# A gated mix of a recurrent memory layer and full attention: its list scheduler rewritten, leftover rows in partition halves, one read for four segments

## The chip, the core and the metric

The kernel runs on one core of a Trainium2 chip. The core has a matrix engine (TensorE; PE for its matmuls and PEld for its weight loads), VectorE (DVE), ScalarE (ACT), GpSimd (POOL), and SyncE (SP), which issues transfers. Engines run their own instruction lists in order and wait for each other through semaphores. PE reads SBUF and writes PSUM, which has eight banks; 16 DMA engines move data between the memory of the chip and SBUF. The metric is the device time of one execution in microseconds (us).

## The reference

Two layers read the same 2048 x 576 input and are mixed row by row with a gate g.

```python
g = sigmoid((x * gate_w).sum(-1, keepdims=True))
# A: 64 segments of 32 rows, each with 8 memory rows in front (h has 40 rows)
for s in range(n_seg):
    h = concatenate([mem, x[:, 32 * s:32 * s + 32]], axis=1)
    q, k, v = h @ Wq, h @ Wk, h @ Wv                  # 32 heads of 128
    scores = where(mask, q @ k.T * scale, -1e9)       # memory rows see all, the rest is causal
    o = (softmax(scores) @ v) @ Wo                    # summed over heads
    mem = o[:, :8]                                    # the next segment's memory
    outs.append(o[:, 8:])
# B: full attention, 32 heads of 18, over all 2048 rows
b = softmax(q @ k.T * scale) @ v @ wo
return g * a + (1 - g) * b
```

Layer A is a recurrence: a segment's first 8 output rows go into the next segment's projections. Layer B has no order among its parts. Operands are bfloat16.

## The kernel before, in words

**Two kinds of work on one set of engines.** The recurrence of A has a long chain of small steps per segment. B consists of 512 *visits*: each takes 128 keys, 512 queries and four heads. In a visit PE multiplies keys and queries in four row tiles of 32 (`sb`, L935; three results in one three-bank tile `sb`, the fourth in a bank `sp`), ScalarE takes the exponentials (`ex`, `ey`, L944 and L948), and PE multiplies them with the values in four column tiles (`ob`, L958). The visits fill the gaps of the recurrence. They are released bit by bit: 48 may run ahead, each of the others depends on a step of a segment.

**A segment of A.** The 40 rows are split into 32 (`CT`: 8 memory rows and 24 inputs) and the last 8 (`LO`), which don't depend on the memory; the latter's projections are made beforehand in *last units* (`la`, L1028 and L1032: turned products, copied as `vl`, stored in `qkd` and `vld` in the chip's memory). For the 32 rows:

1. `Q0`, `K0`, `Q1`, `K1`, `V0`, `V1` (L1317): six half projections, each five steps of four column-tiled matmuls of 512 columns, from `ht` (the rows, turned) and the weights.
2. `eQ`, `eK`, `eV` copy them to `tm` (L540 on DVE or L538 on ACT). `t` (L1407) turns the Q and K halves with a transposing DMA on SP into `tt`, and `ct` (L1416, DVE) copies this into `qk`. `qv` (L1356, SP) and `qc` (DVE or POOL) put V into `v_sb`. `pl` (L1286, POOL) adds the last 8 columns from `xl`, which `ll` (L1277, SP) reads from `qkd`; `lw` (L1295) reads their V rows.
3. For each half: `ph` (L1431 and L1439, PE) adds the mask and multiplies; `xp` (L1449, ACT) takes exponentials; `sm` (L1459 untiled, L1463 column-tiled) sums them; `rc` (L1475, DVE) takes reciprocals; `bc` (L1483) spreads them over the array's rows; `nm` (L1494, DVE) multiplies. The 320 columns (eight heads of 40) go through `sm`, `rc` and `bc` as three chunks of 128 that start at 0, 128 and 192.
4. `po` (L1505, PE, two row tiles of 64: `tall`) multiplies with V; `co` copies to `ot`; `op0` and `op1` (L1197) multiply with Wo; `oc` (L1538, DVE) adds the halves into `obf`.
5. `fo` (L1552 and L1556, PE) turns the 8 memory rows by 12 small matmuls, and `ph<s>` (L1564, DVE) puts them into the other `ht`. The next segment's projections start from there.

**Left-over rows.** The 576 features are four blocks (`NF`) of 144 (`RW`): four full slices of 128 and four rests of 16 (`TR`). A fifth step multiplies all the rests; of the tail weights, `w[1]`, every 32 partitions hold 16 rows for one half of the heads and 16 for the other. The tail of `ht` therefore stands twice (k = `NF` and `NF + 1`), masked with `keep`, which has ones in alternating runs of 16 partitions: `put_x` (L1268) and `put_h` multiply by it, and `w_slice` picks a slice by the half of the heads.

**The order of the instructions** is written by a planner, `Plan`, when the kernel is built. `add` enters a step with its possible engines, a duration, a priority, what it depends on, PSUM banks and buffers that it takes and gives back (tokens), and its transfers. `run` repeatedly takes the engine whose next step can start first; `choose` picks, among steps that can start at nearly the same time, the one of the best rank (priority times a weight, plus `switch` if PE would have to change its tiling). `after` says when a result counts as available, `transfer` when transfers count as landed, and `fetched` what instruction fetch may cost. Where PE would stand idle for longer than a filler takes, a *filler* is put in (`warm_col`, L905, four matmuls of zero weights into `ob`; `warm_full`, L911). `RANKS` has the priorities for four stages of 16 segments; `TURNS` has numbers that reweight all kinds of steps, one per segment from its `Q0` on.

Of the kernel before, what the change touches and what calls it, by code (L numbers as in the profile page):

```python
# [10 lines left out]
FP32 = mybir.dt.float32  # L11
# [8 lines left out]
        "switch": 0.158, "near": 0.011, "early": 0.195, "wait": 0.273, "Q0": 0.964, "K0": 3.412, "Q1": 5.846,  # L20
# [8 lines left out]
        "switch": 0.383, "near": 0.014, "early": 0.178, "wait": 0.273, "Q0": 0.268, "K0": 3.152, "Q1": 5.787,  # L29
# [8 lines left out]
        "switch": 0.088, "near": 0.019, "early": 0.168, "wait": 0.273, "Q0": 0.05, "K0": 4.557, "Q1": 5.756,  # L38
# [8 lines left out]
        "switch": 0.028, "near": 0.019, "early": 0.264, "wait": 0.014, "Q0": 0.05, "K0": 3.865, "Q1": 4.013,  # L47
# [9 lines left out]
TURNS = [  # L57
# [6 lines left out]
]  # L64
FACTORS = (0.02, 0.1, 0.25, 0.4, 0.55, 0.7, 0.85, 1.0, 1.2, 1.5, 1.9, 2.4, 3.0, 4.0, 6.0, 10.0)
KNOBS = ("switch", "near", "early", "wait", "gap", "cool")
# [26 lines left out]
class Op:  # L93


    __slots__ = (
        "engs", "dur", "fn", "deps", "prio", "mode", "take", "give", "tail",
        "eng", "start", "end", "left", "users", "name", "seq", "slots", "dmas", "kb", "use", "pairs", "alt", "form", "waits", "kind",
    )

    def __init__(self, name, engs, dur, fn, deps, prio, mode, take, give, tail):
        self.name, self.fn, self.prio, self.mode = name, fn, prio, mode
# [3 lines left out]
        self.take, self.give, self.tail = take, give, tail  # L106
        self.eng = None
        self.users = []


class Plan:

    LANES = 8
    DRAIN = {"PE": 0.205, "ACT": 0.05, "DVE": 0.05, "POOL": 0.08, "SP": 0.05}
    SWITCH = 0.105
    OVER = {"PE": 0.0, "ACT": 0.1, "DVE": 0.08, "POOL": 0.0, "SP": 0.0}
    CROWDED = (-1.0, 125.0)
    WARM = 0.216  # L120
    BLOCK, FETCH = 128, 3.8
    ARRAY = {"col": 1.0, "row": 1.0, "full": 0.9, "half": 0.3, "tall": 0.35}

    def __init__(self):
        self.ops = []
        self.tokens = {}
        self.now = None
        self.lanes = [0.0] * self.LANES
        self.moved = 0.0
        self.warm = None  # L130
        self.opens, self.closes = set(), set()
        self.count, self.block_end = 45, -9.0
        self.rank, self.stages = RANKS[0], {}
        self.kinds, self.weight = {}, []

    def fetched(self, start, dur, n):

# [21 lines left out]
    def tokens_of(self, name, n):  # L159
        self.tokens[name] = [(0.0, k) for k in range(n)]  # L160

    def slot(self, name, k=0):

        return self.now.slots[name][k]

    def emit(self):
        for op in self.run():
            self.now = op
            op.fn(op.eng)

    def add(
        self, name, engs, dur, fn, deps=(), prio=5.0, mode=None, take=(), give=(), tail=0.0, dmas=0, kb=0.0,
        use=None, pairs=4, alt=None, waits=0.0,
    ):
        op = Op(name, engs, dur, fn, deps, prio, mode, take, give, tail)
        op.dmas, op.kb = dmas, kb
        op.pairs, op.alt, op.form, op.waits = pairs, alt, mode, waits
        op.kind = self.kinds.setdefault(kind_of(name), len(self.kinds))
        op.use = self.ARRAY.get(mode) if use is None else use
        op.seq = len(self.ops)  # L180
        op.slots = {}
        self.ops.append(op)
        return op

    def prefers(self, op):
        return self.liked[op.kind]

    def turn(self, k, stage):
        turn = TURNS[k]
        self.weight = [factor(turn, i) for i in range(len(self.kinds))]  # L190
        self.liked = [turn and (mixed(turn, 2000 + i) & 255) < 100 for i in range(len(self.kinds))]
        self.rank = {x: RANKS[stage][x] * factor(turn, 1000 + i) for i, x in enumerate(KNOBS)}

    def weighed(self, op):
        return op.prio * self.weight[op.kind]

    def after(self, dep, eng):
        end = dep.end + dep.tail
        if dep.eng == eng and dep.tail == 0.0:
            return dep.end - self.OVER[eng]  # L200
        return end + self.DRAIN[dep.eng]

    def run(self):
# [12 lines left out]
        n = len(self.ops)  # L216
        extra = 0
        open_ = False
        recent = []
# [4 lines left out]
        while len(order) < n + extra:  # L224
# [11 lines left out]
            if pick == "PE" and open_ and self.warm is not None:  # L236
                for m in ("col", "full"):
# [3 lines left out]
                    done = sum(d for t, d in recent if t > free["PE"] - 2.5)  # L241
                    if est - free["PE"] < self.WARM + turn + self.rank["gap"] or done > self.rank["cool"]:
                        continue
                    w = Op("warm", "PE", self.WARM, self.warm[m], [], 9.0, m, (), (), 0.0)
                    w.dmas, w.kb, w.slots, w.left, w.use, w.form = 0, 0.0, {}, 0, 1.0, m
                    w.eng, w.start, w.end = "PE", free["PE"], free["PE"] + self.WARM + turn
                    w.end += self.fetched(w.start, self.WARM + turn, 4 if m == "col" else 1)
                    free["PE"], mode = w.end, m
                    recent.append((w.end, self.WARM))
                    order.append(w)  # L250
                    extra += 1
                    pick = None
                    break
                if pick is None:
                    dirty = {"PE"}
                    continue
            waiting_engs = op.engs
            for e in waiting_engs:
                waiting[e].remove(op)
            dirty = set(waiting_engs)  # L260
            dirty.add(pick)
            dur = op.dur[op.engs.index(pick)]
            op.eng, op.start = pick, est
# [1537 lines left out]
```

## Time and profile before

| what | value |
|---|---|
| runs | 1409.65, 1409.65, 1413.18 us; median 1409.65 |
| profiled execution, its span | 1414.1 us |
| instructions | 73462 |
| PE matmuls busy | 1349.3 us, 95% |
| ScalarE, VectorE, GpSimd busy | 1097.6 (78%), 839.4 (59%), 542.2 us (38%) |
| moved by DMA | 130.66 MB, mean 92 GB/s |
| DMA packets, of them under 512 B | 344249, 296751 |
| the first `oc` begins after | some 169 us |

Of the profiled execution, the span from its first to its last instruction is known; it lies 4.4 us above the median of the runs and 0.9 above the longest. The page counts an engine's time while it executes; matmuls overlap and their ends are modelled, so a matmul's printed length isn't the time for which it holds the array. The start of the next group tells that. In the list of waits a line reads: engine, what waited, for what; total us, times, longest.

### The profile page before, as it was taken

The page shows a single profiled execution, that of the slowest core. Times are in us where ns is not written, and L with a number is a line of the kernel's source. Part 1 is how long each engine was busy: PE and PEld are TensorE (multiplying, and loading weights), DVE is VectorE, ACT ScalarE, POOL GpSimd, SP SyncE. Part 2 cuts the span into 40 slices and gives each one's busy share as a digit, 9 for nine tenths or more (in the row PEclk, how much of TensorE's full clock was granted, in tenths as well). Part 3 has the DMA queues.
Part 4 walks back from the last instruction along what each step waited for, and adds up shares of the span by engine and source line. Part 5 has one row for each costly group of instructions (what it writes and reads, how often), then busy time and mean ns, then how long its engine had stood idle before and what let it go on. Part 6 is the DMA issues. An engine that isn't in the chain of part 4 may idle for free. (4 is left out here: it accounts for less than half of the span.)

```text
span 1414.1 us, 73462 instructions
## 1 busy us (share of the span) xinstructions
PE 1349.3 (95%) x32651; PEld 720.9 (51%) x32651; DVE 839.4 (59%) x2027; ACT 1097.6 (78%) x1291; POOL 542.2 (38%) x1172
## 2 busy tenths in 40 slices
PE   7999999999999999999999999999999999999998
PEld 4445445555555545555555544555554444454545
DVE  4443566555666556566656665666655665666657
ACT  3588787787888778888787887788878787788884
POOL 6553444224542344342443325333343324431320
PEclk9999999999999999999999999999999999999999
DMA  7897743334334344333434435333344332333235
GB/s 229 273 319 223 148 84 68 60 70 75 75 66 72 61 76 73 70 65 69 84 66 72 59 68 78 72 60 70 63 101 68 61 56 56 66 61 54 57 64 187
DMA packets 344249, 130.66 MB, mean 92 GB/s; under 512 B 296751, under 2 KB 330279, under 8 KB 343931
## 3 DMA queue, kind: packets, MB, share of 16 engines
q1 hardware_dynamic: 315155, 80.47, 29.7%
q0 software_dynamic: 26624, 43.31, 11.7%
q8 instruction: 255, 4.18, 1.3%
q10 hardware_dynamic: 2152, 2.19, 0.5%
q14 instruction: 63, 0.52, 0.1%
HBM read 52.74 MB, written 31.12 MB: 59 GB/s over the span
## 5 line engine op out<-in xcount | busy, mean ns | idle before, releaser
L944 ACT ACTIVATE etb<-sb 128x1536 bf16<-128x1536 f32 x512 | 743.7, 1453 | 200.2 <-PE sp L935 141.5
L540 DVE CAST tm<-pvv 128x512 bf16<-128x512 f32 x354 | 243.3, 688 | 233.4 <-PE pvv L1317 229.4
L948 ACT ACTIVATE etb<-sp 128x512 bf16<-128x512 f32 x512 | 305.4, 597 | 1.2 <-PE sp L935 0.7
L1317 PEld LDWEIGHTS <-ht 128*32 128x32 bf16 x7680 | 202.2, 96 | 195.5 <-issue 20.9
L935 PE MATMUL sb<-qch,kch 32*128 32x512 bf16 x1536 | 201.2, 385 | 4.1 <-ACT etb L944 1.8
L958 PE MATMUL ob<-etb,vch 128*32 128x512 bf16 x2048 | 202.4, 386 | 1.1 <-DMA vch<-vgd 1.1
L935 PE MATMUL sp<-qch,kch 32*128 32x512 bf16 x512 | 196.6, 384 | 3.8 <-DVE tm L540 3.5
L1197 PE MATMUL acc<-wo,ot 128*32 128x288 bf16 (+1 forms) x6144 | 164.2, 247 | 7.4 <-DVE ot L540 3.7
L1317 PE MATMUL pvv<-wq_m,ht 128*32 128x512 bf16 x2048 | 142.0, 380 | 2.5 <-DVE ht L1564 0.3
L1317 PE MATMUL pvv<-wk_m,ht 128*32 128x512 bf16 x2048 | 141.5, 380 | 1.0 <-DVE ht L1564 0.6
L1317 PE MATMUL pvv<-wv_m,ht 128*32 128x512 bf16 x2048 | 141.5, 380 | 0.1
L1197 PEld LDWEIGHTS <-ot 128*32 128x32 bf16 x6144 | 113.5, 96 | 48.3 <-DVE ot L540 20.6
L935 PEld LDWEIGHTS <-kch 32*128 32x128 bf16 x2048 | 54.0, 91 | 136.4 <-issue 123.7
L540 DVE CAST ot<-pso 128x320 bf16<-128x320 f32 x195 | 89.2, 484 | 55.8 <-PE pso L1505 51.1
L1266 POOL COPY ht<-xg 128x96 bf16<-128x96 bf16 x64 | 18.1, 283 | 252.5 <-PE pvv L1317 241.2
L1416 DVE COPY qk<-tt 128x512 bf16<-128x512 bf16 x256 | 78.6, 309 | 55.2 <-DMA tt<-tm 51.7
L854 POOL DMA_DIRECT2D qch<-qtd x120 | 62.0, 524 | 97.0 <-PE sp L935 91.3
L958 PEld LDWEIGHTS <-vch 128*32 128x32 bf16 x2048 | 53.3, 94 | 77.2 <-issue 65.8
L1449 ACT ACTIVATE et<-psh 128x320 bf16<-128x320 f32 x128 | 56.3, 443 | 39.5 <-PE psh L1439 38.2
L854 POOL DMA_DIRECT2D otd<-stage x124 | 63.2, 517 | 46.2 <-DVE stage L1001 30.3
L1494 DVE TENSOR_TENSOR et<-et,prb 128x320 bf16<-128x320 bf16 x128 | 61.6, 483 | 26.2 <-PE prb L1483 24.9
L540 DVE CAST vl<-pv 128x512 bf16<-128x512 f32 x78 | 53.2, 684 | 35.1 <-PE pv L1028 21.1
(161 smaller groups left out, 1981.1 us busy)
## 6 DMA issues: line engine op xcount, KB each, us to landing
xl<-qkd SPq DMA_DIRECT2D x64, 128.0 KB
v_sb<-tm SPq DMA_DIRECT2D x256, 32.0 KB
qkd<-vl POOLq DMA_DIRECT2D x48, 128.0 KB, 2.7
wo<-in_A_Wo_dram POOLq DMA_DIRECT2D x8, 576.0 KB, 5.5
wq_m<-in_A_Wq_dram POOLq DMA_DIRECT2D x8, 512.0 KB, 6.2
vgd<-vt SPq DMA_DIRECT2D x32, 128.0 KB
wk_m<-in_A_Wk_dram POOLq DMA_DIRECT2D x8, 512.0 KB, 5.9
wv_m<-in_A_Wv_dram POOLq DMA_DIRECT2D x8, 512.0 KB, 8.4
```

What stands on the lines that cost most here:

```text
L540: nc.vector.tensor_copy(out=out_of(), in_=in_of())
L854: dma(out=rows_, in_=pads) if out else dma(out=pads, in_=rows_)
L935: nc.tensor.matmul(sb[:, j, :] if j < 3 else sp[:, :], lhsT=kc[r, o:o + P], rhs=qt_[r, :], start=True, stop=True, tile_position=(32 * j, 0),)
L944: nc.scalar.activation(out=etb[:, 0:3, :], in_=box["sb", gq, kb][:, :, :], func=ACT.Exp, scale=scale_b)
L948: nc.scalar.activation(out=etb[:, 3, :], in_=box["sp", gq, kb][:, :], func=ACT.Exp, scale=scale_b)
L958: nc.tensor.matmul(ob[32 * j:32 * j + 32, :], lhsT=vc[:, o + 32 * j:o + 32 * j + 32], rhs=etb[:, j, :], start=(kb == 0), stop=(kb == NKB - ...
L1197: nc.tensor.matmul(acc[32 * q:32 * q + 32, :], lhsT=o[:, slot, t0:t0 + CT], rhs=wo[:, h, d:d + n], start=(first and s_ == (s_ % 2 if wide ...
L1266: nc.gpsimd.tensor_copy(out=ht[:, 0:NF, M:CT], in_=xg[:, 0:NF, t])
L1317: nc.tensor.matmul(pv[32 * j:32 * j + 32, :], lhsT=ht[:, cc, :], rhs=rw, start=(c == 0), stop=(c == NF), tile_position=(0, 32 * j), skip_g ...
L1416: eng.tensor_copy(out=opened["qk"][:, hf, a, 0:16 * L].rearrange("p (j i t) -> p j i t", i=4, t=L)[:, :, :, 0:CT], in_=box["tt", s, a, hf] ...
L1449: nc.scalar.activation(out=opened["et", hf][:, :], in_=box["psh", s, hf][:, :], func=ACT.Exp, scale=scale_a)
L1494: nc.vector.tensor_tensor(out=et[:, :], in0=et[:, :], in1=box["prb", s, hf][:, :], op=ALU.mult)
```

## The change

**The planner.** `transfer` now covers every transfer, POOL's as well (before, POOL's and one kind on ACT had formulas of their own), with a lag per engine and one rate (`LAG`, `RATES`), an own `lag` or `late` for some steps, and the landing kept as `land`. `after` uses a delay per engine (`LATE`, `OWN`), a `drain` per kind of PE step, and `FAR` for POOL's transfers. A change of tiling no longer lengthens a step; it sets its earliest start. In `choose`, row-tiled and `tall` steps form one class (`APART`): entering it costs `switch`, staying in it earns `join`; ahead of a row-tiled step, a `tall` one that can start within `lead` is preferred if tokens are left for both (`room`). Many durations of steps are new (`ph` 0.36 for 0.41, `bc` 0.151 for 0.24, `po` 0.2 for 0.14, `sb` 0.222 for 0.3). Three reweightings are made per segment, at `Q0`, `ph0` and `op0` (the pattern `TURN`), from a new list `TURNS` of some 190 numbers. The RANKS priorities stay.

**The steps.** The three chunks of `sm`, `rc` and `bc` are 107 wide, from 0, 107 and 213. The 16 left-over rows of two neighbouring blocks are now adjacent in memory (`row0` shifts odd blocks' slices by 16), so rests are 32 rows; those for a group of 512 columns stand in one half of the partitions, those for the other in the other half. `put_x` and `put_m0` copy halves and don't multiply; `fold` issues 16 matmuls; `keep` has ones by halves. `ll` reads `qkd` for four segments at once (64 reads become 16) into one `xl` buffer of four times the size, and `put_l` makes four copies for two. The rings of K and V chunks have four buffers, not five. Fillers stream `ident`, not a tile of ones.

```diff
 class Plan:
     LANES = 8
-    DRAIN = {"PE": 0.205, "ACT": 0.05, "DVE": 0.05, "POOL": 0.08, "SP": 0.05}
-    SWITCH = 0.105
+    LATE = {"ACT": 0.055, "DVE": 0.055, "POOL": 0.06, "SP": 0.03}
+    OWN = {"PE": 0.0, "ACT": -0.1, "DVE": 0.03, "POOL": 0.0, "SP": 0.0}
     OVER = {"PE": 0.0, "ACT": 0.1, "DVE": 0.08, "POOL": 0.0, "SP": 0.0}
-    CROWDED = (-1.0, 125.0)
+    LAG = {"SP": 0.66, "ACT": 0.66, "POOL": 1.25}
+    FAR, LANDED = 0.235, 0.025
+    RATES = ((300.0, 0.8), (220.0, 0.55))
+    EARLY = 125.0
+    SWITCH = 0.103
+    APART = ("row", "tall", "quad")
...
     def transfer(self, op):
-        wait, after = (0.6, 0.5) if op.end < self.CROWDED[1] else (0.9, 1.0)
         step = (op.end - op.start) / op.dmas
+        lag = self.LAG[op.eng] if op.lag is None else op.lag
+        rate, after = self.RATES[0 if op.end < self.EARLY else 1]
         for j in range(op.dmas):
             issued = op.start + (j + 1) * step
-            self.moved = max(self.moved, issued + wait) + op.kb / op.dmas / (290.0 if op.end < 150.0 else 300.0)
-            self.lanes.append(max(self.moved + after, self.lanes[-1]))
+            self.moved = max(self.moved, issued + lag) + op.kb / op.dmas / rate
+            op.land = self.moved + after + op.late
+            if op.eng != "POOL":
+                self.lanes.append(max(op.land, self.lanes[-1]))
         self.lanes = self.lanes[-self.LANES:]
-        op.tail = self.lanes[-1] - op.end
...
-    def after(self, dep, eng):
-        end = dep.end + dep.tail
-        if dep.eng == eng and dep.tail == 0.0:
-            return dep.end - self.OVER[eng]
-        return end + self.DRAIN[dep.eng]
+    def after(self, dep, op, e):
+        far = self.FAR if e == "POOL" and op.dmas else 0.0
+        if dep.land is not None:
+            return dep.land + self.LANDED + far
+        if dep.eng == e:
+            return dep.end + self.OWN[e] + far
+        return dep.end + (dep.drain if dep.eng == "PE" else self.LATE[dep.eng]) + far
...
                 if op.form != mode:
-                    dur += self.SWITCH
+                    est = max(est, free["PE"] + self.SWITCH)
...
         def rank(f):
             op = f[1]
-            switch = 0.0 if e != "PE" or mode in (op.mode, op.alt and op.alt[0]) else self.rank["switch"]
+            switch = 0.0
+            if e == "PE" and op.mode in self.APART and op.mode != mode:
+                switch = -self.rank["join"] if mode in self.APART else self.rank["switch"]
+            elif e == "PE" and op.goes_on:
+                switch = -self.rank["hold"]
             return (self.weighed(op) + switch, op.seq)
         got = min(near, key=rank)
+        if e == "PE" and got[1].mode == "row" and mode not in self.APART:
+            lim = got[0] + self.rank["lead"]
+            ahead = [f for f in found if f[1].mode in self.APART[1:] and f[0] <= lim and self.room(f[1], got[1], lim)]
+            if ahead:
+                return min(ahead, key=rank)
...
-    NKR, NVR, NQR = 5, 5, 2
+    NKR, NVR, NQR = 4, 4, 2
...
+    def row0(c):
+        return RW * c + TR * (c % 2)
     def rows(t, c):
-        return t[RW * c:RW * c + P, :]
+        return t[row0(c):row0(c) + P, :]
...
+    def tail_rows(w, f0):
+        return (f0 // 512 + w[2]) % 2
     def w_slice(w, c, f0, n):
         if c < NF:
             return w[0][:, f0 // WB, c, f0 % WB:f0 % WB + n], c
-        f1 = f0 % (HD // 2)
-        return w[1][:, f1:f1 + n], NF + f0 // (HD // 2)
+        f1 = f0 // 1024 * 512 + f0 % 512
+        return w[1][:, f1:f1 + n], NF + tail_rows(w, f0)
...
         def put_x(e, s=s, ht_i=ht_i):
-            for k in (NF, NF + 1):
-                nc.gpsimd.tensor_tensor(
-                    out=ht[:, k, M:CT], in0=xg[:, NF, t], in1=keep[:, k:k + 1].to_broadcast([P, CT - M]), op=ALU.mult
-                )
+            for k in range(2):
+                nc.gpsimd.tensor_copy(out=ht[64 * k:64 * k + 64, NF + k, M:CT], in_=xg[64 * k:64 * k + 64, NF, t])
...
-        ll = add(f"ll{s}", "SP", 0.5, ld_l, [opening, *last_done[sq, False]], prio=0.75, take=("xl",), dmas=1, kb=350)
+        if s % 4 == 0:
+            ll = add(f"ll{s}", "SP", 0.5, ld_l, [opening, *last_done[sq, False]], prio=0.75, take=("xl",), dmas=1, kb=512)
...
                 t_ = add(
-                    f"t{a}{hf}.{s}", "SP", 1.25, turn, [ev_a], prio=RANK[f"t{hf}"], take=("tt",),
-                    give=(("tm", ev_a, 0),), dmas=1, kb=128,
+                    f"t{a}{hf}.{s}", "SP", 1.3, turn, [ev_a], prio=RANK[f"t{hf}"], take=("tt",),
+                    give=(("tm", ev_a, 0),), dmas=1, kb=128, lag=0.02, late=0.4,
                 )
...
-            CH = (0, P, W8 - P)
+            CN = 107
+            CH = (0, CN, W8 - CN)
...
-                            pr[32 * i:32 * i + 32, o:o + P],
-                            lhsT=box["rq", s, hf][:, 2 * k + i // 2:2 * k + i // 2 + 1].to_broadcast([P, 32]),
-                            rhs=ident[:, :], start=True, stop=True, tile_position=(0, 32 * i), skip_group_check=True,
+                            pr[32 * i:32 * i + 32, o:o + CN],
+                            lhsT=box["rq", s, hf][0:CN, 2 * k + i // 2:2 * k + i // 2 + 1].to_broadcast([CN, 32]),
+                            rhs=ident[0:CN, 0:CN], start=True, stop=True, tile_position=(0, 32 * i), skip_group_check=True,
...
-            if re.match(r"Q0\.\d+\.0$", op.name):
+            if self.TURN.match(op.name):
                 turns += 1
                 self.turn(turns, stage)
```

More of the change, by code (lines that the diff above doesn't have):

```diff
@@ L136, in fetched, with turn, weighed @@
+    def turn(self, k, stage):
+        turn = TURNS[k] if k < len(TURNS) else 0
+        self.weight = [factor(turn, i) for i in range(len(self.kinds))]
+        self.liked = [turn and (mixed(turn, 2000 + i) & 255) < 100 for i in range(len(self.kinds))]
+        self.rank = {x: RANKS[stage][x] * factor(turn, 1000 + i) for i, x in enumerate(KNOBS)}
+    def weighed(self, op):
+        return op.prio * self.weight[op.kind]
     def fetched(self, start, dur, n):
@@ L223, in run @@
         self.turn(0, 0)
-        while len(order) < n + extra:
+        while left:
             for e in dirty:
@@ L235, in run @@
             est, op = best[pick]
-            if pick == "PE" and open_ and self.warm is not None:
+            if pick == "PE" and open_:
+                filled = False
                 for m in ("col", "full"):
@@ L314, in run, with room @@
         return order
+    def room(self, a, b, at):
+        for t in set(a.take):
+            if sum(x[0] <= at for x in self.tokens[t]) < a.take.count(t) + b.take.count(t):
+                return False
+        return True
     def choose(self, e, ops, now, mode):
@@ L645 @@
         x_tile(n)
-    for c in range(NF):
-        load_tails(c)
+    for b in range(2):
+        load_tails(b)
     for part in range(3):
```

368 lines of the change are left out of this document (156 added, 212 removed), and 22 rows, old and new, of the table TURNS.

## The prediction

> **What bounds the kernel now.** I began with the page: its span, the busy shares, and the chain that ended last, by lines.
>
> ```profile
> span 1414.1 us, 73462 instructions
> PE 1349.3 (95%) x32651; PEld 720.9 (51%) x32651; DVE 839.4 (59%) x2027; ACT 1097.6 (78%) x1291; POOL 542.2 (38%) x1172
> ...
> PE pvv L1317 7%; PE acc L1197 3%; DMA tt<-tm 3%; PE sb L935 2%; PE ob L958 2%; PE po L1724 1%; DVE tm L540 1%; PE pso L1505 1%; DMA v_sb<-tm 1%; ACT etb L944 1%; PE ob L905 1%; DVE v_sb L1356 0%; DVE qk L1416 0%; DMA wk_m<-a_dram 0%; PE prb L1483 0%
> ```
>
> PE leads, and the one transfer of weight on the chain is `tt<-tm`, a segment's turned queries and keys. Then I cut the span into stages. The first fence holds the stage of segments that have leftover `la` units to fill in, and the stage without them: the stretch, PE's busy time (and instructions), then those of PEld, DVE, ACT and POOL, granted clock, DMA. The second counts `oc` (L1538, one to a segment), the third the filler matmuls (L905, four to a group).
>
> ```profile
> 170.00:1120.00 950.00, 915.38 (x24123) 496.87 (x24111) 576.93 (x1385) 759.82 (x910) 374.21 (x794) 1.00 0.38 71
> 1120.00:1363.00 243.00, 230.80 (x6063) 115.82 (x6059) 149.13 (x364) 196.07 (x226) 76.96 (x170) 0.99 0.32 57
> ```
>
> ```profile
> 170.00:1120.00 950.00, 14.94 (x49) 1.00 0.38 71
> 1120.00:1363.00 243.00, 3.99 (x13) 0.99 0.32 57
> ```
>
> ```profile
> 170.00:1120.00 950.00, 26.27 (x280) 7.44 (x280) 1.00 0.38 71
> 1120.00:1363.00 243.00, 18.05 (x220) 4.82 (x212) 0.99 0.32 57
> ```
>
> A segment takes 950/49 = 19.4 us, later 243/13 = 18.7. PE idles 950 - 915.4 = 34.6 and 243 - 230.8 = 12.2 us. Fillers are idle time in disguise: 280/4 = 70 and 220/4 = 55 groups. How long a group holds the array, and what a change of tiling costs, stands in the PE timeline.
>
> ```profile
> 1045.34 0.39 PE L1317 MATMUL pvv<-wq_t,ht 128*32 128x512 bf16 x4
> 1045.55 0.61 PE L1317 MATMUL pvv<-wk_m,ht 128*32 128x512 bf16 x8
> 1046.09 0.39 PE L935 MATMUL sb<-qch,kch 32*128 32x512 bf16 x3
> ...
> 1046.41 0.61 PE L1317 MATMUL pvv<-wk_m,ht 128*32 128x512 bf16 x8
> ```
>
> A group of four is followed by the next after 1045.55 - 1045.34 = 0.21 us (the printed 0.39 overlaps). The two groups from 1045.55 are through at 1045.97; the row-tiled `sb` starts at 1046.09, and 0.32 later column-tiled work goes on: 0.1 us for each change of tiling. So fillers stand for 125 x 0.21 = 26 us, and the **pool of avoidable PE time** in both stages is 34.6 + 12.2 + 26 = 73 us of 1193. Without idle time and fillers a segment needs 19.4 - (34.6 + 14.7)/49 = 18.4 us of PE early, 18.7 - (12.2 + 11.6)/13 = 16.9 late: 1.5 us less work, yet the period fell by 0.7. Late segments are partly paced by their own chain of steps, early ones by PE. What ends PE's idle time, longest first (total, times, longest):
>
> ```profile
> PE psh L1439 <- DVE qk L1416: 9.8, 18, 2.1
> PE prb L1483 <- DVE rq L1475: 7.7, 15, 1.8
> PE ptx L597 <- DMA xn<-in_A_x_dram: 5.0, 3, 3.7
> PE acc L1197 <- DVE ot L540: 3.7, 12, 1.0
> PE sp L935 <- DVE tm L540: 3.5, 4, 1.9
> PE pso L1505 <- DVE et L1494: 2.7, 9, 0.7
> ```
>
> **The change part by part.** Durations are those of the profiled execution with its span of 1414.1 us; the runs took 1409.65, 1409.65 and 1413.18, so the span is 4.4 above their median. The terms are small against either, and I set their sum on 1409.65 unscaled.
>
> *Narrower chunks in `sm`, `rc`, `bc`.* `bc` streams three chunks of 107 columns in place of 128. The price of columns:
>
> ```profile
> 1034.06 0.40 PE L1028 MATMUL pv<-xL,wq_m 128*128 128x128 bf16 x4
> 1034.30 0.22 PE L1028 MATMUL pv<-xL,wq_t 128*128 128x128 bf16 x1
> 1034.35 0.39 PE L1028 MATMUL pv<-xL,wq_m 128*128 128x128 bf16 x4
> ```
>
> Five matmuls of 128 columns take 0.29 us, 0.058 each; 63 columns less save 0.028 us, x128 (two per segment) = **-3.6 us**, on PE and on the way from reciprocal to `nm`. Against it: where `sm` runs untiled, it now loads 107 weight columns, not 128. The group over the whole run (mean 97 ns a load), and one place:
>
> ```profile
> L1459 PEld LDWEIGHTS <-et 128*128 128x128 bf16 x120 | 6.1, 97 | 4.7 <-ACT et L1449 3.0 <-issue 0.9
> ```
>
> ```profile
> 1055.44 0.18 PEld L1459 LDWEIGHTS <-et 128*128 128x128 bf16 x3
> ```
>
> Three loads overlap into 0.18 us. Should they no longer overlap, they take 3 x 0.097 = 0.29, 0.11 more, x40 groups = 4.4; the other end is 0. I take **+1**, nearer the row as it stands. [...]
>
> *`fold`* issues 16 small matmuls, not 12, on the chain that ends a segment. In the timeline further down, 12 small `pss` matmuls and a change of tiling take 1039.02 - 1038.76 = 0.26 us, 0.013 each without the change: 4 x 0.013 x 63 = 3.3 us, or 0 where `ht` is not what comes last. I take the middle, **+1.7**.
>
> *Left-over rows in halves; `xl` for four segments at once.* On GpSimd the two products of `lh` become copies of 64 partitions, and `pl` makes four copies, not two; SP issues 16 reads of 512 KB, not 64 of 128 KB.
>
> ```profile
> L1286 POOL COPY qk<-xl 128x256 bf16<-128x256 bf16 x128 | 50.2, 409 | 53.4 <-PE psh L1439 41.2 <-DMA xl<-qkd 5.2 <-PE pss L1463 2.4
> ```
>
> ```profile
> qkd<-vl POOLq DMA_DIRECT2D x48, 128.0 KB, 2.7
> wo<-in_A_Wo_dram POOLq DMA_DIRECT2D x8, 576.0 KB, 5.5
> ```
>
> Half-size copies cost at most as much each as now, 2 x 0.41 us more per segment, and at least nothing in sum; POOL is busy 38%, and `pl` has the time from one segment's last `psh` to the next one's first. A read may land after 5.5 us, not 2.7, but is released in a fourth segment's `pl` and needed a segment (19 us) later: 0, hidden by that slack. If the slack were gone, 16 x 2.8 = 45 us is the far end; a gain is bounded by the 5.2 us that POOL waits for `xl` now. On SP's queue 48 issues fewer free time that transposes may use, and the one of 512 KB may stand ahead of a transpose; I count both as 0. The K and V rings shrink from five chunks to four, one head group: a chunk comes free 12 visits before its next use, and about seven visits go to a segment (`sb` in 512 visits, 48 of them ahead), so some 30 us for a load of four small reads: 0. In the prologue there are fewer small loads, but the same bytes; the 5.0 us that `ptx` waits there bound the gain, and I take 0.
>
> *The scheduler.* What its some 190 draws (three turns a segment, not one) make of the order can't be read off a profile. Two things can. First, it sets `pso` (two tiles of 64 rows) next to `sb`.
>
> ```profile
> 1038.76 0.24 PE L1463 MATMUL pss<-bsel,et 128*32 128x2 bf16 x12
> 1039.02 0.37 PE L1505 MATMUL pso<-et,v_sb 64*128 64x40 bf16 x16
> 1039.32 0.39 PE L935 MATMUL sb<-qch,kch 32*128 32x512 bf16 x3
> ...
> 1040.88 0.37 PE L1505 MATMUL pso<-et,v_sb 64*128 64x40 bf16 x16
> 1041.18 0.43 PE L1197 MATMUL acc<-wo,ot 128*32 128x288 bf16 x8
> ```
>
> One `pso` here stands next to `sb` already, the other between column-tiled work. Side by side, three changes are paid, not four: 0.1 us for each `pso` not yet paired, 0 to 12.8 us for 128. If half are paired, as here, and half of the rest follow, **-3 us**. Second, the table of durations by which waits are placed is corrected. I credit it with the PE waits for results of VectorE whose times the plan can know, the `rq`, `ot`, `tm` and `et` rows: 7.7 + 3.7 + 3.5 + 2.7 = **-17.6 us**; fillers and waits behind landings stay. Its ends are the whole pool, -73, and +42 from the first rival.
>
> Sum: -3.6 + 1 + 1.7 - 3 - 17.6 = -21.5, so **1388 us**, with a range of its own of 1375 to 1400.
>
> **The rivals.** *Landings come later than the new plan allows: slower.* Before, a transpose counts as landed 1.25 + 0.9 + 0.43 + 1.0 + 0.05 = 3.6 us after its issue begins; after, 1.3 + 0.02 + 0.58 + 0.55 + 0.4 + 0.03 = 2.9. Pieces of the chain, from issue to landing, and VectorE's waits for them:
>
> ```profile
> 1033.33 4.08 DMA tt<-tm
> ...
> 1201.01 5.08 DMA tt<-tm
> ```
>
> ```profile
> DVE qk L1416 <- DMA tt<-tm: 51.7, 60, 3.2
> ```
>
> VectorE waits for 60 of 256 landings even now, and 18 `psh` wait for its copy (9.8 us). PE works in order: behind a `psh` that waits stand `sb` and the projections, and ScalarE waits for those. If `psh` comes 0.7 us sooner and all 60 late landings reach PE, that is 60 x 0.7 = 42 us, against 21.5 gained: 1430. It decides from 21.5/0.7 = 31 such landings on. For it: landings of 4 to 5 us, beyond either allowance. Against it: today 42 of the 60 waits end without a `psh` that waits, covered by other PE work. Between 31 and 60 lies 1410 to 1430; I write 1420.
>
> *The segment's own chain sets the pace: no change.* For it, the late stage, whose period follows its work only by half. Then the waits that are filled come back as fillers, the two scheduler terms fall away and -0.9 is left: 1409. Against it, early segments (49 of 62) hold 18.4 us of PE work in 19.4.
>
> *More of the pool is won.* Half of it, 37 us, with the other terms -3.6 + 1 + 1.7 - 3: 1369. Early segments would then take about 18.9 us, just above the 18.7 at which the late ones run, so this is near the floor. For it: in both stages no wait in the list above is longer than 2.1 us, some ten groups of other work.
>
> *The change doesn't do what it says.* If rank and tokens still keep `pso` from `sb`, -3 falls away: 1391, inside the forecast.
>
> **How the numbers follow.** Forecast (1375 to 1400) 0.45; more of the pool 0.25; chain sets the pace 0.12; late landings 0.18. A measurement of this kernel can tell some 0.3% from no change, 4 us. Faster has the first two and a little of the third: 0.72; same 0.10; slower 0.18. For 8 in 10 the range reaches down to 1360, below the half pool, and up to 1416, into the slower case.
>
> **What would show it.** Right: filler groups and PE idle between 170 us and the last `oc` fall together by about 20 us, early period near 19.0; `prb` is 0.028 us shorter per group; `pso` starts or ends at an `sb` more often. Wrong: `psh` waits for `qk` 30 us or more, not 9.8 (late landings); idle falls but L905 rises above its 588 matmuls (chain); POOL's wait for `xl` or PE's for `kch` grows beyond a few us (the slack I counted on is not there).

## The result, and the profile after

The changed kernel took **1392.61 us** (median of four runs, 1390.1 to 1395.66); the kernel before, on the same chip, took 1411.41 (1409.65 to 1415.81). The ratio is **0.9876, with 0.9842 to 0.9911**: faster by some 19 us. The forecast was 1388, with 1360 to 1416.

Top of the page of the kernel after: span, PE's busy time and instructions, DMA packets.

```profile
span 1393.9 us, 73578 instructions
...
PE 1340.9 (96%) x32621; PEld 717.4 (51%) x32638; DVE 795.4 (57%) x1925; ACT 1125.4 (81%) x1359; POOL 573.9 (41%) x1327
...
DMA packets 245082, 130.67 MB, mean 94 GB/s; under 512 B 197583, under 2 KB 231111, under 8 KB 244763
```

The same bytes move in 99,000 packets fewer. This is the line of the page before:

```profile
DMA packets 344249, 130.66 MB, mean 92 GB/s; under 512 B 296751, under 2 KB 330279, under 8 KB 343931
```

Where the 20.2 us between the two spans went is seen from `oc`, one to a segment. Its rows before and after give count, shortest/median/longest ns, and the start of the first and of the last:

```profile
L1538 DVE TENSOR_TENSOR obf<-acc,sum x64: 269/307/309, 168.8 to 1384.7; 128x144 bf16<-128x144 f32 x64
```

```profile
L1511 DVE TENSOR_TENSOR obf<-acc,sum x64: 289/308/310, 163.6 to 1363.7; 128x144 bf16<-128x144 f32 x64
```

The first comes 5.2 us sooner. From first to last it is 1215.9 us before and 1200.1 after: 15.8 less over 63 intervals, 19.30 and 19.05 us each. The first 49 intervals, the prediction's early stage, took 19.40 us each and now take 19.13 (from 163.6 to 1101.1), the next 13 took 18.67 and take 18.28 (to 1338.8). What follows the last is 29.4 and 30.2 us.

A cut between `oc`s that holds 62 of them, like the 1193 us of the prediction's two stages together, stands in the next fences of the kernel after: all engines as there, and the filler matmuls (now L908).

```profile
164.00:1339.00 1175.00, 1140.65 (x30161) 609.00 (x30168) 686.10 (x1656) 996.31 (x1215) 492.71 (x1135) 1.00 0.34 69
```

```profile
164.00:1339.00 1175.00, 47.94 (x528) 13.18 (x528) 1.00 0.34 69
```

For 62 segments PE idles 1175 - 1140.65 = 34.4 us, before 46.8: 12.4 less. The fillers went up, from 125 groups to 528/4 = 132, by 7 x 0.21 = 1.5 us. The pool of avoidable time, 73 us, is now 34.4 + 132 x 0.21 = 62.

PE's waits in the kernel after (total, times, longest):

```profile
PE psh L1410 <- DVE qk L1387: 11.8, 20, 1.4
PE ptx L593 <- DMA xn<-in_A_x_dram: 4.5, 2, 3.8
...
PE prb L1456 <- DVE rq L1448: 2.9, 7, 0.7
...
PE sb L938 <- ACT etb L947: 1.8, 6, 0.6
PE pso L1478 <- DVE et L1467: 1.6, 7, 0.3
...
PE acc L1198 <- DVE ot L533: 0.7, 3, 0.3
...
PE psh L1402 <- DVE tm L533: 0.4, 1, 0.4
```

The four rows for VectorE's results (`rq`, `et`, `ot`, `tm`) came to 17.6 us and are now 2.9 + 1.6 + 0.7 = 5.2: the `tm` row of before was `sp`'s, and none of its kind is listed any more (the 0.4 above is `psh`'s, which was 1.0). In a second profile of the same kernel, that of the first experiment, the four come to 6.6. The wait behind the landing of `tt`, through `qk`, did not fall: 9.8 before, 11.8 now.

### The profile page after: what moved, and what is told of

It is laid out like the page before. It is cut to its first block, busy times and chain, and to the rows that moved or that the text cites. A ratio compares the mean times of both kernels' runs of the same rounds, so it can differ in the third digit from the quotient of the medians.

```text
span 1393.9 us, 73578 instructions
## 1 busy us (share of the span) xinstructions
PE 1340.9 (96%) x32621; PEld 717.4 (51%) x32638; DVE 795.4 (57%) x1925; ACT 1125.4 (81%) x1359; POOL 573.9 (41%) x1327
## 5 line engine op out<-in xcount | busy, mean ns | idle before, releaser
L533 DVE CAST tm<-pvv 128x512 bf16<-128x512 f32 x344 | 237.4, 690 | 238.0 <-PE pvv L1316 234.4
L1316 PE MATMUL pvv<-wq_m,ht 128*32 128x512 bf16 x2048 | 145.0, 380 | 2.4 <-DVE wo L664 1.3
L1316 PE MATMUL pvv<-wk_m,ht 128*32 128x512 bf16 x2048 | 146.1, 380 | 0.9 <-issue 0.4
L1316 PE MATMUL pvv<-wv_m,ht 128*32 128x512 bf16 x2048 | 144.4, 380 | 0.1
L1387 DVE COPY qk<-tt 128x512 bf16<-128x512 bf16 x256 | 76.7, 301 | 58.8 <-DMA tt<-tm 56.7
L1355 POOL COPY v_sb<-tm 32x512 bf16<-32x512 bf16 x68 | 41.8, 615 | 155.1 <-DVE tm L533 152.7
L533 DVE CAST ot<-pso 128x320 bf16<-128x320 f32 x160 | 74.9, 486 | 50.2 <-PE pso L1478 47.1
L1288 POOL COPY qk<-xl 128x128 bf16<-128x128 bf16 x256 | 66.6, 296 | 40.1 <-PE psh L1410 24.3
L1267 POOL COPY ht<-xg 128x96 bf16<-128x96 bf16 x64 | 18.7, 292 | 146.0 <-PE pvv L1316 138.5
```

The costliest lines, as they stand in the source:

```text
L533: nc.vector.tensor_copy(out=out_of(), in_=in_of())
L1288: nc.gpsimd.tensor_copy(out=opened["qk"][:, f, a, 0:16 * L].rearrange("p (u h t) -> p u h t", h=4, t=L)[:, :, :, CT:L], in_=xl[:, f, a, :, ...
L1316: nc.tensor.matmul(box["pvv", s, n][32 * j:32 * j + 32, :], lhsT=opened["ht", ht_i][:, cc, :], rhs=rw, start=(c == 0), stop=(c == NF), til ...
L1355: move(out=opened["v_sb"][64 * (j // 2):64 * (j // 2) + CT, o:o + 512], in_=tm[32 * j:32 * j + CT, :],)
L1387: eng.tensor_copy(out=opened["qk"][:, hf, a, 0:16 * L].rearrange("p (j i t) -> p j i t", i=4, t=L)[:, :, :, 0:CT], in_=box["tt", s, a, hf] ...
```

## The experiments

The theory: the order of the instructions, by the corrected durations, brings the time, and the edits to the steps bring nothing. Its rivals: the steps bring it; or the landings of the transposes, which the new plan counts on sooner, take some of it back.

**The kernel after, once more**, as a reference beside the next three.

> The changed kernel itself, beside the others of this call on the same chip. Both theories: 1390 to 1396 us, ratio to before 0.984 to 0.991. It is the mark against which the three below are read. Theory A (order): the gain of 18.8 us comes from the order of the instructions, the steps give a few us at most. Theory B (steps): narrower chunks, lighter GpSimd work and the other layout give most of it.

It took 1395.63 us, ratio 0.988 (0.9849 to 0.9911). The kernel after comes out at 1392.6 and 1395.6, its single runs between 1385 and 1397. The kernel before took 1408.8 to 1413.7 us beside the various runs, which were on several chips; so variants are compared by their ratios to the kernel before beside them, and a single difference of less than 5 us is within the scatter.

**The steps without the order.** The halves, the narrow chunks, the fold of 16 and the fillers' stream were put into the kernel before, whose planner, turns, reads of `xl` and rings stay.

```diff
-            CH = (0, P, W8 - P)
+            CN = 107
+            CH = (0, CN, W8 - CN)
...
-            for k in (NF, NF + 1):
-                nc.gpsimd.tensor_tensor(
...
+            for k in range(2):
+                nc.gpsimd.tensor_copy(out=ht[64 * k:64 * k + 64, NF + k, M:CT], in_=xg[64 * k:64 * k + 64, NF, t])
```

> The kernel before with its own planner and order, but with the changed steps: chunks of 107, left-over rows in halves (copies of halves in lh, fold of 16 matmuls). xl reads, rings, fillers' number and planner as before. Theory A: -3.6 for bc, +1 to +2 for fold, +2 for 40 untiled sm groups: 1408 to 1412 us, ratio 0.997 to 1.001. Theory B: 1393 to 1400 us, ratio 0.988 to 0.993.

It took 1412.07 us, ratio 1.0016 (0.9998 to 1.0033). The stage keeps before's length, and the fillers keep their number:

```profile
L1544 DVE TENSOR_TENSOR obf<-acc,sum x64: 269/308/309, 166.5 to 1381.4; 128x144 bf16<-128x144 f32 x64
```

```profile
L913 PE MATMUL ob<-ident,nil 128*32 128x512 bf16 x588 | 51.4, 382 | 0.0
```

So the steps bring nothing by themselves; the whole gain needs the new order with its rings of four buffers, the merged reads of `xl`, or both.

**Chunks of 128 again, and only the loads of 128 again.** The first sets all three chunks of the kernel after back to 128 columns.

```diff
-            CN = 107
+            CN = P
```

> The changed kernel in its own order, with chunks of 128 columns again in sm, rc and bc (nothing else differs). Theory A: bc costs 0.028 us more in each of 128 groups, +3.6 us, and the untiled sm gets its overlapping weight loads back, 59 groups x 0.05 = -3 us: between 0 and +4 us against e1. Theory B (the time from the first prb matmul to the next work fell by 9.8 us in all, 30.8 to 21.0): +8 to +10 us.

The second keeps `rc` and `bc` narrow, and only the untiled `sm` loads 128 weight columns (the tile `et` is 22 columns wider, filled with zeros).

```diff
-    ps[0:CN, 2 * k:2 * k + 2], lhsT=opened["et", hf][:, o:o + CN], rhs=bsel[:, :], start=True, stop=True
+    ps[:, 2 * k:2 * k + 2], lhsT=opened["et", hf][:, o:o + P], rhs=bsel[:, :], start=True, stop=True
```

> The changed kernel in its own order; only the untiled sm loads 128 weight columns instead of 107 (columns past the chunk give rows that nothing reads; the exponentials' tile is 22 columns wider). If a load of 107 columns is slow because it is not 128 wide, the group's matmuls follow at 0.026 us and not at 0.050, loads take 97 ns and not 128, and 59 groups x 0.05 us are worth up to -3 us. Rival: the loads hide behind other work, 0 us within 0.2%.

They took 1389.02 us (0.9851, 0.983 to 0.9873) and 1386.39 us (0.9841, 0.9812 to 0.9869). The first was expected at 0 to +4 us against the kernel after beside it (1395.63) and came out 6.6 below. The second was run again, since its interval met that of the kernel after:

> The kernel of the run with 128-column loads in the untiled sm (1386.39 us, ratio 0.9841 with 0.9812 to 0.9869, against 0.988 with 0.9849 to 0.9911 for the kernel after beside it), in five more rounds, because the two intervals overlap. If the narrow untiled load costs the kernel after what the group's span says or more (59 groups of 0.055 us, 3.3 us, and the waits behind it): 1384 to 1390 us and a ratio whose interval stays below 0.9866, the middle of the runs of the kernel after and of its 256-byte pieces in four issues. If not: 1391 to 1397 us.

It took 1389.47 us, ratio 0.9852 (0.9814 to 0.989); by its own condition that does not settle it. The weight loads themselves are clear. The groups of the kernel after (the profile of the first experiment) and of the second variant, busy us and mean ns of one before the last bar:

```profile
L1431 PEld LDWEIGHTS <-et 128*107 128x107 bf16 x177 | 14.0, 128 | 5.6 <-ACT et L1420 2.5 <-issue 2.0
```

```profile
L1432 PEld LDWEIGHTS <-et 128*128 128x128 bf16 x177 | 10.0, 97 | 6.0 <-ACT et L1421 3.0 <-issue 2.2
```

And three such loads in the timeline of the kernel after; three of 128 columns took 0.18 us in the place that the prediction shows, and as much in the first variant (median of 59 groups):

```profile
599.99 0.23 PEld L1431 LDWEIGHTS <-et 128*107 128x107 bf16 x3
```

A load of 107 columns takes 128 ns where one of 128 columns takes 97. The new order also runs 59 groups of `sm` untiled (177 loads), 40 before (120): 59 x 0.05 = 3 us of PE time. In whole kernels, the ratios of the three measurements with wide loads (0.9851, 0.9841, 0.9852) lie below all three with narrow ones in the final order (0.9876, 0.988, and 0.9866 further down), on average by 0.26%, some 3.7 us. That is the size of the loads, but the intervals overlap, so the sign is likely and not proved. On these numbers the kernel after with wide loads is the fastest of the versions that give the right result.

**The reads of `xl` apart again.** The kernel after, with each read of 512 KB issued as four reads of 128 KB, one per segment and so in pieces of 64 bytes as before the change; all four stand at the place of the one, and order and buffers stay.

```diff
-            dma(
-                out=xl[:, :, :],
-                in_=qkd[sq][:, :, si * 4 * LO:(si + 4) * 4 * LO].rearrange("u p f -> p u f"),
-            )
+            for i in range(4):
+                dma(
+                    out=xl[:, :, 4 * LO * i:4 * LO * i + 4 * LO],
+                    in_=qkd[sq][:, :, (si + i) * 4 * LO:(si + i + 1) * 4 * LO].rearrange("u p f -> p u f"),
+                )
```

> The changed kernel in its own order, but each of the 16 reads of 512 KB is issued as four reads of 128 KB with pieces of 64 bytes at the same place, into the same buffer: 64 issues and some 98,000 packets more, as before the change. Theory (the reads are needed a segment later, so neither size nor packets matter): within 4 us of the changed kernel. Rival (small pieces hold up the transposes on the same queue): 5 us or more slower, with longer landings of tt.

It took **1401.71 us**, ratio 0.9937 (0.9918 to 0.9956): by the ratios 8 to 9 us longer than the kernel after (0.9876 and 0.988). Two things differ: 98,000 small packets, and three more issues on SyncE's queue each time. The next kernel keeps the four issues, but splits the read by units, so that the pieces stay 256 bytes.

```diff
+            for i in range(4):
+                dma(
+                    out=xl[:, 4 * i:4 * i + 4, :],
+                    in_=qkd[sq][4 * i:4 * i + 4, :, si * 4 * LO:(si + 4) * 4 * LO].rearrange("u p f -> p u f"),
+                )
```

> The kernel after, with each 512 KB read of last columns (xl) again issued as four reads of 128 KB, but split by units of columns and not by segments, so the pieces stay 256 bytes (the run that split it by segments made 64-byte pieces, took 1401.7 us and had 344154 packets against 245082). It keeps the four issues on SyncE and leaves out the small packets. If the small packets are what the merged read removes: 1391 to 1397 us, the psh wait for DVE qk back near 12 us. If the extra issues on SyncE, in front of the transposes, are: 1399 to 1403 us, psh wait 17 to 20 us.

It took **1392.92 us**, ratio 0.9866 (0.984 to 0.9891). So the pieces are it, not the issues; only PE's wait for `qk`, 15.5 us, lies between the 12 and the 17 to 20 that were expected of the two cases. The queue's line on the page (packets, MB, share of 16 engines), VectorE's wait for landings, and PE's wait behind it, first with 64-byte pieces, then with 256-byte ones:

```profile
q1 hardware_dynamic: 315139, 80.47, 30.8%
...
DVE qk L1388 <- DMA tt<-tm: 70.0, 76, 2.8
...
PE psh L1411 <- DVE qk L1388: 19.4, 25, 2.0
```

```profile
q1 hardware_dynamic: 216835, 80.47, 27.1%
...
DVE qk L1388 <- DMA tt<-tm: 65.6, 77, 2.0
...
PE psh L1411 <- DVE qk L1388: 15.5, 24, 1.2
```

The same megabytes hold the 16 DMA engines 3.7% of the span longer, 54 us in all (431 and 376 us), 0.8 us for each of the 64 reads. PE's wait for `qk` is 4 us longer, which is part of the 9. Between the first and the last `oc` the two differ by 5.6 us, 4.7 of them idle time of PE (42.4 against 37.6 us). The rest has no row: the first `oc` stands at 166.7 with small pieces and 162.3 with wide ones, but it lies between 160.4 and 166.7 in all kernels with this order and its turns, so that part may be scatter.

**How near the landings are to the path.** Two kernels move the landing of `tt` both ways in the order after. In the first the transpose is a plain copy of the same 128 KB, so queries and keys are left unturned.

```diff
-                    nc.sync.dma_start_transpose(out=tt[:, :, :], in_=box["tm", s, "QK"[a] + str(hf)][:, :])
+                    nc.sync.dma_start(out=tt[:, :, :].rearrange("p i t -> p (i t)"), in_=box["tm", s, "QK"[a] + str(hf)][:, :])
```

> The changed kernel in its own order, with each of the 256 transposing transfers replaced by a plain transfer of the same 128 KB (the queries and keys are left unturned, so the output is another; a plain transfer takes about 0.4 us to issue, not 1.2, and lands sooner). It measures what waiting for landings costs in this order. Theory (landings still set part of the chain: psh waits 11.8 us for their copies): 8 to 15 us faster than the changed kernel. Rival (the order covers the landings): within 4 us of it.

In the second, a store of the same tile to a scratch buffer in DRAM stands ahead of each transpose, work that the kernel does not need.

```diff
+                    dma(out=pad[:, :], in_=box["tm", s, "QK"[a] + str(hf)][:, :])
                     nc.sync.dma_start_transpose(out=tt[:, :, :], in_=box["tm", s, "QK"[a] + str(hf)][:, :])
```

> The changed kernel in its own order, with a plain store of 128 KB into a scratch tensor of the chip's memory ahead of each of the 256 transposing transfers, on the same queue, so that each lands some 0.5 to 1.0 us later. Theory of the slower rival (thin margins): most of the 256 come late for psh or for the copies ahead of it, +40 us or more against the changed kernel, and psh's wait for qk rises from 11.8 to 40 us or more. Theory that the order has room: +15 us at most, psh's wait under 25 us.

The plain copies took 1369.24 us (0.9711, 0.969 to 0.9732), the later landings 1549.58 us (1.102, 1.0952 to 1.1087). VectorE's wait for the landing (56.7 us in 77 places in the kernel after) and PE's behind it, plain copies first:

```profile
DVE qk L1387 <- DMA tt<-tm: 19.2, 24, 2.0
...
PE psh L1410 <- DVE qk L1387: 3.4, 6, 1.0
```

```profile
DVE qk L1389 <- DMA tt<-tm: 229.0, 185, 4.4
...
PE psh L1412 <- DVE qk L1389: 77.9, 64, 4.0
...
PE prb L1458 <- DVE rq L1450: 23.9, 20, 3.5
```

Sooner landings are worth some 24 us by the ratios, more than the 8 to 15 expected; later ones cost 155: (1549.58 - 1394)/256 = 0.6 us of kernel time for each delayed transpose. Not all of that is waiting. These are PE's busy time and its instructions, then the other engines, the granted clock and DMA, from the first to the last `oc`, in the kernel after and with later landings:

```profile
163.64:1363.72 1200.08, 1164.23 (x30697) 621.10 (x30696) 699.10 (x1688) 1016.47 (x1240) 495.66 (x1141) 1.00 0.35 72
```

```profile
162.12:1520.03 1357.91, 1207.34 (x30697) 634.82 (x30696) 702.33 (x1688) 1022.36 (x1240) 494.08 (x1141) 0.96 0.38 87
```

PE idles 150.6 us for 35.9, 115 more, or 0.45 us for each transpose. The same 30697 matmuls keep it busy 43 us longer, at a granted clock of 0.964 for 0.997 in that stretch; an estimate from the clocks alone is 1164 x (0.997/0.964 - 1) = 40.

The price of the delay is an upper end, for the store also occupies SyncE and the queue: 0.39 us for its issue, and a wait for earlier stores to land. These are the rows of SyncE's queue in that kernel (shortest/median/longest ns; total, times, longest):

```profile
L1379 SPq DMA_DIRECT2D pad<-tm x256: 319/394/1363, 132.2 to 1505.2; - x128
```

```profile
SPq L1379 <- DMA pad<-tm: 47.4, 74, 3.7
```

In the same way the plain copy also frees SyncE: its issue takes 513 ns, that of a transpose 1217.

```profile
L1378 SPq DMA_DIRECT2D tt<-tm x256: 464/513/1366, 134.4 to 1326.5; - x128
```

```profile
L1378 SPq DMA_TRANSPOSE tt<-tm x256: 1188/1217/2573, 135.8 to 1352.6; - x128
```

The two kernels show that the path transpose, `qk`, `psh` has little slack left in this order; they do not split the landing from the issue.

**No fillers.** The matmuls of the two filler steps (zero weights, nothing is added to the result) are left out; the order of the rest stays.

> The changed kernel in its own order without its fillers (169 groups of matmuls that add zeros are left out; the output is the same). Theory: fillers are idle time in disguise, so PE's idle time grows by about 169 x 0.21 = 35 us and the time stays within 4 us of the changed kernel. Rival 1: fillers hold the array when real work is ready, 5 to 15 us faster. Rival 2: the granted clock falls in the gaps, slower by 5 us or more with a clock under 0.99 between the first and the last oc.

It took 1400.49 us, ratio 0.9934 (0.9912 to 0.9956): some 8 us slower than the kernel after by the ratios, though the fillers hold the array for 168 x 0.21 = 35 us there (the printed 57 overlap). First the row of the filler matmuls in the kernel after (the profile of the first experiment), then PE's busy time without them, then the longest waits, with one for ScalarE that was 1.8:

```profile
L908 PE MATMUL ob<-ident,nil 128*32 128x512 bf16 x672 | 57.0, 379 | 0.0
```

```profile
PE 1315.7 (94%) x31945; PEld 711.7 (51%) x31962; DVE 793.3 (57%) x1925; ACT 1124.7 (80%) x1359; POOL 573.2 (41%) x1327
```

```profile
PE psh L1404 <- DVE qk L1381: 16.1, 22, 1.9
PE sb L932 <- ACT etb L941: 9.4, 22, 1.0
PE prb L1450 <- DVE rq L1442: 8.1, 16, 1.1
```

So fillers do stand in time that PE has to wait out anyway, as the prediction counted them: from the first to the last `oc` PE now idles 65.6 us, not 35.9, 30 us more, which is what the 144 groups that stood there come to. Why leaving them out costs something is not settled. The mean granted clock was 0.987 to 0.990 in all five runs, and 0.995 to 1.0 in the ten of the kernel after; from 0.996 to 0.990, as in the two profiles, that could be up to 8 us, an estimate from the clocks alone. But in this profile the clock is low ahead of the first `oc` (0.95), which comes at 165.3, only 0.7 to 1.7 us later than in the two profiles of the kernel after. From there to the last `oc` the clock is 0.996, against 0.997 and 0.999, and the stretch is still 2.8 to 6.1 us longer.

**No turns.** The 193 numbers that reweight the new scheduler's priorities are set to zero, in the kernel after.

```diff
-TURNS = [
-    1248037, 9999345, 9165946, 5014097, 8907777, 316325, 9650527, 9032474, 9414537, 3013551, 4101324, 8422068,
...
+TURNS = [0] * 193 + []
```

> The kernel after, with all of the scheduler's 193 turns set to zero, so that the list scheduler's own costs and ranks give the order and no searched perturbation. Theory that the gain lies in the order found by the search over draws of late landings: much slower, 1480 to 1600 us, and no faster than the same kernel with before's scheduler (next run). Rival that the one model of the transfers by itself gives a better order: within 3% of the kernel after, and faster than the next run by 16 us or more.

The same was done with the old scheduler's 65 numbers:

> The new steps in before's scheduler (the kernel of the run of the steps alone, 1412.07 us), with its 65 turns set to zero. Theory of the search: 1480 to 1600 us, like the run before it or below it. Rival of the model: slower than the run before it by 16 us or more, as 1412 is slower than 1395.

One correction to that text: the kernel that ran has the old steps as well, that is, it is the kernel before with its turns set to zero; the steps alone were worth 1.0016 above. The two took 1535.53 us (1.0867, 1.0838 to 1.0895) and 1521.61 us (1.076, 1.0732 to 1.0789). PE's busy time and the fillers, first the new scheduler, then the old:

```profile
PE 1426.5 (93%) x36387; PEld 752.3 (49%) x36387; DVE 807.4 (53%) x1967; ACT 1119.3 (73%) x1341; POOL 562.3 (37%) x1303
...
L891 PE MATMUL ob<-ident,nil 128*32 128x512 bf16 x1944 | 150.9, 388 | 1.4 <-issue 1.4
```

```profile
PE 1405.3 (92%) x35957; PEld 750.5 (49%) x35957; DVE 813.6 (53%) x1951; ACT 1119.6 (74%) x1349; POOL 557.2 (37%) x1190
...
L898 PE MATMUL ob<-unit,nil 128*32 128x512 bf16 x1368 | 105.9, 384 | 0.0
```

Without turns the new scheduler has 486 groups of fillers and 1531.1 - 1426.5 = 104.6 us of idle PE (168 and 53.0 in the kernel after), and its order is 14 us slower than the old one's. So the new model and rules do not by themselves make the better order; with the turns found for it, it is the better. Zero is one point among many for each scheduler, and the new one has three turns to a segment where the old had one: whether the judgement over draws, the number of turns or the model makes the found order better is not told apart.

## Why the prediction was right, and where not

The sum, -21.5, stands against -18.8 by the medians (1411.41 to 1392.61). The terms fared less well than the sum, and that it came so near is in part luck: the reads of `xl` and the prologue, put at 0, made up for what the waits and `pso` fell short. From the runs: the steps in the old order are worth +2 us (1.0016, between -0.3 and +4.7), where the prediction's three terms for them make -0.9; the new order with the 64-byte reads brings a further 0.9937 - 1.0016 = -0.8%, **-11 us**; the wide reads bring **-8 to -10**. That is some -17 to -19. The order counts here with two edits that no run takes apart from it, the rings of four buffers and the four copies of `pl`; of the rings, no wait of PE for `kch` or `vch` is listed after (1.4 and 1.1 us before).

*Waits for VectorE's results, -17.6.* The waits fell as said, at two thirds of the size: the four rows lost 11 to 12 us, and idle PE lost 12.4 in the stage. That the corrected durations did it is argued and not shown: the new order also puts fewer copies on VectorE, whose busy time fell from 839 to 795 us. "Fillers and waits behind landings stay" held: `psh` waits 11.8 us for 9.8, the fillers rose a little.

*`pso` next to `sb`, -3.* This got nothing. Counted in the traces, 64 of the 128 `pso` stand next to an `sb` before (29 ahead of one, 35 behind one) and 64 after (56 and 8). The order turned the pairs round instead of making more: the rival that rank and tokens keep them apart was right on this step. All changes of tiling together are some 1305 before and 1330 after.

*The chunks, -3.6 + 1.* The narrower `bc` is on the page as priced:

```profile
L1456 PE MATMUL prb<-ident,rq 107*32 107x107 bf16 x1536 | 41.7, 213 | 3.3 <-DVE rq L1448 2.9
```

In the order of starts a group of 12 takes 0.026 us less, 0.028 was said. The load was mis-sized: +1 was "nearer the row as it stands", and the loads come to some 3 us, with the number of untiled groups, taken as 40, at 59 because the order is free to choose the form. With it and what waits behind, the edit is about zero or a loss. In the traces a load of the untiled `sm` takes 128 ns with 107 columns and 97 with 128, three of them 0.23 and 0.18 us; these two widths are the only ones it ran with, and why the narrower load takes longer was not shown.

*`fold`, +1.7.* In the order of starts its matmuls hold PE, up to the next other work, for 10.9 us in all before, 12.8 with the new steps in the old order and 11.1 after: between 0.2 and 1.9 us, as the prediction's ends had it.

*`xl`, 0.* This is the term that failed. The prediction asked whether the reads land in time, and they do: POOL waits for one once, at the start, in the kernel after. That is more than the 5.2 us of before, as the prediction's sign of missing slack has it, but it stands at 149 us, ahead of the first segment's `oc`, which came sooner all the same.

```profile
POOL qk L1288 <- DMA xl<-qkd: 12.2, 1, 12.2
```

It did not ask what the reads do to others on the same queue. 64-byte pieces hold the DMA engines 0.8 us longer per read, beside the transposes whose landings have little slack; to make them wider was worth 8 to 10 us. "A gain is bounded by the 5.2 us that POOL waits for `xl`" was the wrong bound: that row shows who waits for the read, not whom the read delays. The page before had the hint, 296,751 packets under 512 bytes. From the two queue lines, one small packet more costs an engine, as an estimate, 54 us x 16/98,304 = 8.8 ns.

*The prologue, 0.* The first `oc` came 5.2 us sooner; the steps in the old order have it at 166.5, the ten profiles with the new order between 160.4 and 166.7. Some 4 us may be real, and no run shows which edit brings it.

*The rivals.* Late landings did not decide: `psh` waits 11.8 us in 20 places, not 30 us. But the margin is as thin as it was drawn: a later landing costs 0.6 us of the kernel each, 0.45 of it idle time of PE. The chain setting the pace (fillers above 588) is seen in part: 588 to 672 over the whole run, while idle time fell more; but the 18.7 us of the late segments were no floor, for these take 18.3 now. Half the pool was not won, 11 of 73 us.

The unfilled work of PE in 62 segments is also about 7 us smaller (1193 - 73 = 1120, 1175 - 62 = 1113). `prb` is 126 x 0.026 = 3.3 of that; the rest is open, for the two stretches do not hold quite the same visits and last units (447 and 455 `sp`).

## What to carry to other kernels

Before calling a transfer hidden, ask not only who waits for it but which transfers share its queue: the count of small packets on the page gives the hint, and here the pieces' size was worth nearly as much as the new order (8 to 10 us and 11). Credit a better plan with the waits whose ends it can know, and not with all of them: here two thirds went. A rewritten scheduler is judged by the order it ends with, searched; its unsearched order says little.

## What the runs showed of the hardware beyond what was expected

Reads of the same bytes in 64-byte pieces, not 256-byte ones, cost 0.8 us more on all 16 DMA engines per 128 KB, while four issues in place of one cost nothing that can be seen (0.9866 against 0.9876 and 0.988). The untiled weight loads of `sm` take 128 ns with 107 columns and 97 with 128. A transpose in the DMA takes SyncE 1217 ns to issue, a plain copy of the same tile 513. And 35 us of filler matmuls could be left out without any gain; without them the granted clock was lower in every run (0.987 to 0.990, not 0.995 to 1.0). Where later landings made PE idle 115 us more, the clock fell from 0.997 to 0.964 and the same matmuls took 43 us longer.
